# One attention block's backward pass: K read in one pass instead of two

## The chip, the cores and the metric

The kernel runs on one core of a Trainium2 chip. The core has a matrix engine (PE, with its weight loads shown apart as PEld), a vector engine (DVE), a scalar engine (ACT), a general engine (POOL) and a sync engine (SP) that issues most transfers; 16 DMA engines move data between the memory of the chip and the two on-core memories, SBUF (128 partitions) and PSUM (8 banks, the only place to which PE writes). The metric is the device time of one execution in microseconds, lower is better.

## The reference

One decode block, forward and gradient: layer norm, attention of one query per head against a cache, output projection, residual; then layer norm, a relu MLP, residual. There are B = 2 batches, H = 32 heads, Sk = 4096 cached positions, Dh = 128, D = 640, Dff = 1728, all bf16.

```python
q = (layernorm(x) @ wq).reshape(B, 1, H, Dh).transpose(0, 2, 1, 3)
scores = einsum("bhqd,bhkd->bhqk", q, k_cache) * Dh ** -0.5
o = einsum("bhqk,bhkd->bhqd", softmax(scores), v_cache)
h = x + o.transpose(0, 2, 1, 3).reshape(B, 1, H * Dh) @ wo
out = h + relu(layernorm(h) @ w1) @ w2
# returned: out, and the gradients of <out, grad_out> for x, k_cache, v_cache, wq, wo, w1, w2
```

For one batch and head write e for the unnormalised softmax weights, P = e / sum(e), go for the gradient that reaches o. The gradients of the attention are

- gV = P go' (4096 x 128),
- gs = P * (V go - dot) * scale, where dot = sum(P * (V go)), and gK = gs q' (4096 x 128),
- gq = K' gs, from which the gradients of wq and of x follow.

go depends on the whole forward pass of its batch and on the MLP's backward pass, so gV and gK can't be begun while the batch's heads are still in their forward pass. K and V of one head are 1 MiB each, gK and gV as well; there are 64 (batch, head) pairs.

## The kernel before, in words

All of K, V, gK and gV are handled pair by pair as tiles of 128 partitions x 32 columns of 128 numbers ("natural" layout, one 1 MiB transfer each). Products that sum over Dh need the transposed tile: 32 PE transposes in four groups of 8 into a PSUM bank (tag tps, two banks), each group copied to SBUF by DVE (L302) or ACT (L304). Products that sum over positions use the natural tile as the weights.

- First pass, all 64 pairs (lines 326 to 418): load K, transpose it, 32 one-column score products (L350), a softmax for four heads at a time, load V of the four heads, 32 one-column products with V (L414) that give o. Loads are issued on SP's queue.
- Change-over of a batch (`middle_gen`, lines 420 to 555): output projection, layer norm, MLP, its backward pass, and go for all heads. It is a generator, of which a few steps are run after each pair. Its long DVE work is rows of product-and-sum over wo (L549), w2 (L501) and w1 (L531).
- Second pass, all 64 pairs (lines 561 to 667): load V, transpose it, 32 one-column products with go (L593); load K again, form gs, 32 one-column products that give gq (L645); gV and gK by one DVE multiplication each (L661, L665) and a store each from POOL's queue. gV and gK have two buffers each.
- Weight gradients and the gradient of x: partly beside the second batch's second pass (`fin_wgrads_gen`), partly after the last pair (lines 817 to 847; the products of L679 are copied by L683 and L685 and stored from POOL).

```python
414    nc.tensor.matmul(ocol_ps[:, h:h + 1], lhsT=Vt[:, sc, :], rhs=P_bf[:, bh, sc:sc + 1],
                        start=(sc == 0), stop=(sc == NSC - 1))
602    nc.sync.dma_start(out=Kt[:], in_=A_k_cache[b, h].rearrange("(p sc) d -> p sc d", sc=NSC))
645    nc.tensor.matmul(gq_ps[:, h:h + 1], lhsT=Kt[:, sc, :], rhs=gs_bf[:, sc:sc + 1],
                        start=(sc == 0), stop=(sc == NSC - 1))
767    for i in range(NPAIR + LD + 1):     # first pass: pair i loads, i-1 transposes, i-2 scores, ...
792    for i in range(NPAIR + 5):          # second pass, after the whole first pass
```

The order of the work on each engine's queue is fixed when the program is built: a planner takes the instructions by their place in the program and by when it expects their inputs and buffers to be ready, so that neighbouring stages mix. A tile with n buffers can be written again when all readers of an earlier one are done; the queue that issues the transfer waits for that.

Of the kernel before, what the change touches and what calls it, by code (L numbers as in the profile page):

```python
# [12 lines left out]

EPS = 1e-5
DBG = None

MID_STEPS_PER_HEAD = 2
FIN_STEPS_PER_HEAD = 3
NDVE_FRAC = 0.72
P1_EVAC_DVE = 0.5  # L20
P2_EVAC_DVE = 0.5


def _dbg(nc, name, src_ap):
    if DBG is not None and name in DBG:
        nc.sync.dma_start(out=DBG[name], in_=src_ap)


def _chunks(total, size):
    out = []  # L30
    s = 0
    while s < total:
        n = min(size, total - s)
        out.append((s, n))
        s += n
    return out
# [3 lines left out]
def kernel(  # L40
# [26 lines left out]
    assert Sq == 1  # L67
    assert Dh == 128
    assert H * Dh == HD, "only Hq == Hkv (rep 1) supported"
    assert D % 128 == 0 and Sk % 128 == 0 and HD % 128 == 0  # L70
    assert 1 <= B <= 4
    ND = D // 128
    NSC = Sk // 128
    NF_full = Dff // 128
    F_rem = Dff - NF_full * 128
    NF = NF_full + (1 if F_rem else 0)
    PB = [32 * b for b in range(B)]
    NP = PB[-1] + 1
    SCALE = float(Dh) ** -0.5
    SCALE_BF = 0.08837890625  # L80
    eps_bf = 1.0013580322265625e-05
    NDVE = max(1, min(NSC, int(round(NSC * 0.6875))))
    GT = 8

    D_ch = _chunks(D, 512)
    F_ch = _chunks(Dff, 512)
    HD_ch = _chunks(HD, 512)

    def f_kc(c):
        return 128 if c < NF_full else F_rem  # L90

    const = ctx.enter_context(tc.tile_pool(name="const", bufs=1))
    rows = ctx.enter_context(tc.tile_pool(name="rows", bufs=1))
    cols = ctx.enter_context(tc.tile_pool(name="cols", bufs=1))
    small = ctx.enter_context(tc.tile_pool(name="small", bufs=4))
    rtmp = ctx.enter_context(tc.tile_pool(name="rtmp", bufs=1))
    ps = ctx.enter_context(tc.tile_pool(name="ps", bufs=1, space=bass.MemoryType.PSUM))
    PSB = {"tps": 2, "sps": 2, "tiny": 2, "rowps": 1, "bigps": 1, "acc": 1}
# [4 lines left out]
                            fill=1.0, base=0, pattern=[[-1, 128]], channel_multiplier=1)  # L103
    ident_f32 = const.tile([128, 128], FP32)
    nc.gpsimd.memset(ident_f32[:], 0.0)
    nc.gpsimd.affine_select(out=ident_f32[:], in_=ident_f32[:], compare_op=ALU.not_equal,
# [6 lines left out]
    x_bf = rows.tile([NP, D], BF16)  # L113
# [30 lines left out]
    for b in range(B):  # L144
        nc.sync.dma_start(out=x_bf[PB[b]:PB[b] + 1, :], in_=A_x[b, 0:1, :])
        nc.sync.dma_start(out=g_bf[PB[b]:PB[b] + 1, :], in_=grad_out[b, 0:1, :])

# [730 lines left out]
```

## Time and profile before

| | |
|---|---|
| median of 3 runs | 1195.17 us (1194.96 to 1195.88) |
| the profiled execution | 1193.57 us, span 1191.8 us |
| mean granted PE clock | 0.609 |
| packets moved | 439.78 MB, mean 369 GB/s |

Columns of a group's row: line, engine, operation, output <- inputs, shapes, count, then busy us and mean ns of one, then the engine's idle time before them and what ended it. In a row of a stretch: its bounds and length, busy time of each engine (number of instructions), the granted PE clock, the share of time in which the DMA engines were busy, GB/s. A row of a transfer gives its size and the median time from issue to landing. A row of waits gives who waited for whom, the total, how often, and the longest.

### The profile page before, as it was taken

To read this page: it belongs to the slowest core of one execution; us is meant where nothing else is said; L and a number is where in the kernel's file an instruction comes from. 1 tells how busy PE (TensorE), PEld (TensorE's weight loads), DVE (VectorE), ACT (ScalarE), POOL (GpSimd) and SP (SyncE) were. 2 spreads that over 40 slices of the span, in tenths; PEclk is the share of its full clock that TensorE was granted. 3 is DMA by queue.
4 is the path that set the end of the run, shared out by engine and by line. 5 is a ranking of instruction groups with operands and counts; after the bars stand their busy time and mean duration, and the time that the engine had idled before them with its cause. 6 is when DMAs were issued, how large, how long until landed. Compare 5 with 4: busy or idle time off the path is not lost.

```text
span 1191.8 us, 31531 instructions
## 1 busy us (share of the span) xinstructions
PE 783.3 (66%) x14044; PEld 705.3 (59%) x14044; DVE 772.4 (65%) x1622; ACT 372.3 (31%) x533; POOL 109.3 (9%) x206
## 2 busy tenths in 40 slices
PE   3966787788876667868666667545675555665245
PEld 3856677787865657767555566445664455655221
DVE  5322233235367957586987999565677788966694
ACT  1322343244333213333232223423543421322023
POOL 0100000000000000001110011010121222111111
PEclk9767778687767767555555555555755555555565
DMA  8899989988867779999999999999999999999714
GB/s 342 315 401 379 372 356 386 380 346 344 351 255 288 313 271 408 424 425 423 426 423 406 385 417 425 382 407 391 423 401 424 413 421 410 412 425 414 324 74 178
DMA packets 62097, 439.78 MB, mean 369 GB/s; under 512 B 7332, under 2 KB 7336, under 8 KB 10888
## 3 DMA queue, kind: packets, MB, share of 16 engines
q1 hardware_dynamic: 38248, 278.94, 58.1%
q0 software_dynamic: 23712, 158.81, 32.2%
q8 instruction: 110, 1.80, 0.6%
q14 instruction: 27, 0.22, 0.0%
HBM read 288.59 MB, written 149.13 MB: 367 GB/s over the span
## 4 chain that ended last, share of the span: by engine, by line
issue 22%; DMA 15%; PE 12%; DVE 12%; POOL 4%; ACT 3%; POOLq 0%; SPq 0%; ACTq 0%; DVEq 0%
DMA Vt<-in_A_v_cache_dram 7%; PE t_ps L299 6%; DMA stage<-in_A_wq_dram 5%; DVE junk L549 3%; DMA Kt<-in_A_k_cache_dram 2%; POOL out_dram L746 2%; DVE gK L665 2%; ACT VTsb L304 2%; DVE gV L661 1%; POOL out_dram L663 1%; POOL out_dram L667 1%; PE t_ps L718 1%; DVE VTsb L302 1%; PE gq_ps L645 1%; PE o_ps L679 1%
## 5 line engine op out<-in xcount | busy, mean ns | idle before, releaser
L299 PE MATMUL t_ps<-ident_bf,Vt 128*128 128x128 bf16 x2048 | 249.8, 302 | 146.9 <-ACT VTsb L304 92.8
L299 PEld LDWEIGHTS <-Vt 128*128 128x128 bf16 x2048 | 205.2, 139 | 174.6 <-issue 127.1
L299 PE MATMUL t_ps<-ident_bf,Kt 128*128 128x128 bf16 x2048 | 194.7, 255 | 63.5 <-DMA Kt<-in_A_k_cache_dram 33.4
L304 ACT COPY KTsb<-t_ps 128x1024 bf16<-128x1024 bf16 x128 | 126.2, 1013 | 241.9 <-PE t_ps L299 203.1
L299 PEld LDWEIGHTS <-Kt 128*128 128x128 bf16 x2048 | 157.3, 116 | 74.5 <-issue 35.7
L302 DVE COPY KTsb<-t_ps 128x1024 bf16<-128x1024 bf16 x128 | 88.3, 690 | 165.1 <-PE t_ps L299 163.4
L304 ACT COPY VTsb<-t_ps 128x1024 bf16<-128x1024 bf16 x128 | 129.1, 1012 | 179.6 <-PE t_ps L299 160.2
L665 DVE TENSOR_TENSOR gK<-qb,gsp 128x4096 bf16<-128x4096 bf16 x64 | 146.6, 2290 | 19.5 <-DMA out_dram<-gK 19.4
L661 DVE TENSOR_TENSOR gV<-gob,Pp 128x4096 bf16<-128x4096 bf16 x64 | 146.4, 2287 | 3.0 <-ACT gob L584 1.6
L302 DVE COPY VTsb<-t_ps 128x1024 bf16<-128x1024 bf16 x128 | 87.4, 691 | 88.8 <-PE t_ps L299 74.1
L350 PE MATMUL s_ps_g<-qcol,KTsb 128*128 128x1 bf16 x2048 | 87.8, 166 | 3.6 <-ACT KTsb L304 1.5
L645 PE MATMUL gq_ps<-gs_bf,Kt 128*128 128x1 bf16 x2048 | 69.5, 166 | 28.9 <-DVE gs_bf L628 25.3
L593 PEld LDWEIGHTS <-VTsb 128*128 128x128 bf16 x2048 | 73.2, 106 | 24.9 <-issue 22.7
L645 PEld LDWEIGHTS <-Kt 128*128 128x128 bf16 x2048 | 68.7, 105 | 32.3 <-issue 26.1
L593 PE MATMUL gp_ps<-gocol_bf,VTsb 128*128 128x1 bf16 x2048 | 73.3, 167 | 20.9 <-DVE gs L623 20.3
L414 PE MATMUL ocol_ps<-P_bf,Vt 128*128 128x1 bf16 x2048 | 62.5, 165 | 37.1 <-DMA Vt<-in_A_v_cache_dram 25.5
L414 PEld LDWEIGHTS <-Vt 128*128 128x128 bf16 x2048 | 58.5, 101 | 42.4 <-DMA Vt<-in_A_v_cache_dram 26.9
L350 PEld LDWEIGHTS <-KTsb 128*128 128x128 bf16 x2048 | 77.9, 100 | 7.5 <-ACT KTsb L304 3.5
L579 ACT CAST qb<-qb_ps 128x128 bf16<-128x128 f32 x64 | 17.1, 266 | 166.6 <-PE qb_ps L576 159.7
L663 POOL DMA_DIRECT2D out_dram<-gV x64 | 34.3, 536 | 369.8 <-DVE gV L661 258.1
L549 DVE CUSTOM_DVE_ANT_0 junk<-wo_t,gh_bcast 128x640 bf16<-128x640 bf16 x64 | 53.2, 831 | 0.5
L667 POOL DMA_DIRECT2D out_dram<-gK x64 | 34.4, 537 | 202.9 <-DVE gK L665 63.6
(180 smaller groups left out, 806.0 us busy)
## 6 DMA issues: line engine op xcount, KB each, us to landing
Kt<-in_A_k_cache_dram SPq DMA_DIRECT2D x128, 1024.0 KB, 13.9
Vt<-in_A_v_cache_dram SPq DMA_DIRECT2D x128, 1024.0 KB, 12.4
out_dram<-gV POOLq DMA_DIRECT2D x64, 1024.0 KB, 11.1
out_dram<-gK POOLq DMA_DIRECT2D x64, 1024.0 KB, 12.7
out_dram<-otile POOLq DMA_DIRECT2D x45, 160.0 KB, 10.0
wq_t<-in_A_wq_dram SPq DMA_DIRECT2D x1, 5120.0 KB, 15.3
wo_t<-in_A_wo_dram POOLq DMA_DIRECT2D x1, 5120.0 KB, 31.9
stage<-in_A_wq_dram SPq DMA_DIRECT2D x5, 1024.0 KB, 13.0
```

What stands on the lines that cost most here:

```text
L299: nc.tensor.transpose(t_ps[:, j, :], nat_tile[:, sc, :], ident_bf[:])
L302: nc.vector.tensor_copy(out=dst_sb[:, g0:g0 + gn, :], in_=t_ps[:, 0:gn, :])
L304: nc.scalar.copy(out=dst_sb[:, g0:g0 + gn, :], in_=t_ps[:, 0:gn, :])
L350: nc.tensor.matmul(s_ps[:, j, sc:sc + 1], lhsT=KTsb[:, sc, :], rhs=qcol[:, b, h:h + 1], start=True, stop=True)
L414: nc.tensor.matmul(ocol_ps[:, h:h + 1], lhsT=Vt[:, sc, :], rhs=P_bf[:, bh, sc:sc + 1], start=(sc == 0), stop=(sc == NSC - 1))
L549: nc.vector.tensor_tensor_reduce(out=junk[:], in0=wo_t[:, h, :], in1=gh1_bcast[:], scale=1.0, scalar=0.0, op0=ALU.mult, op1=ALU.add, accum ...
L593: nc.tensor.matmul(gp_ps[:, sc:sc + 1], lhsT=VTsb[:, sc, :], rhs=gocol_bf[:, b, h:h + 1], start=True, stop=True)
L645: nc.tensor.matmul(gq_ps[:, h:h + 1], lhsT=Kt[:, sc, :], rhs=gs_bf[:, sc:sc + 1], start=(sc == 0), stop=(sc == NSC - 1))
L661: nc.vector.tensor_tensor(out=gV[:].rearrange("p s (a two) -> p s a two", two=2), in0=gob3, in1=P32[:, :, None, :].to_broadcast([128, NSC, ...
L663: nc.gpsimd.dma_start(out=gV_dram, in_=gV[:])
L665: nc.vector.tensor_tensor(out=gK[:].rearrange("p s (a two) -> p s a two", two=2), in0=qb3, in1=gss[:, :, None, :].to_broadcast([128, NSC, ...
L667: nc.gpsimd.dma_start(out=gK_dram, in_=gK[:])
```

## The change

- **K is read once.** With M = V'diag(e)K (128 x 128) and u = K'e, the query gradient is gq = scale * (M' go - dot * K'e) / sum(e). Both are formed in the first pass, when K and V of the pair are in SBUF together. DVE multiplies K by e in two halves into rows of 130 numbers, the 129th being e itself; 32 products of 129 columns give M and o at once, 32 one-column products give u. M / sum(e) is kept in SBUF (tag MT, 46 buffers). The second pass no longer loads K, and gq is 32 one-column products per batch in `middle_gen`. The softmax is done for each head by itself.
- **Batches are interleaved.** Batch 0's change-over runs beside the first heads of batch 1's first pass, and as soon as its go is known, batch 0's second pass runs round by round with batch 1's first pass. What is left of batch 0's second pass runs beside batch 1's change-over, and the weight gradients run beside batch 1's second pass.
- **Buffers and queues.** V has four buffers that both passes share. gK and gV share three. wq comes in four pieces; wo, w1 and w2 are loaded by SP in six pieces between the heads. Weight gradients are outer products on PE through one PSUM bank (tag mid) and are stored from SP.
- **Layer norms and the vectors of the block** lie in columns over 128 partitions instead of in one row.

The core of the new code ("..." where lines are left out; `transpose_group` is 8 transposes and one copy, by DVE if its last argument is true and else by ACT; `matvec_group` is 8 one-column products):

```python
def load_k(i):
    Kt = work.tile([128, NSC, 128], BF16, tag="K", bufs=3, name="Kt")
    nc.sync.dma_start(out=Kt[:], in_=natural(A_k_cache, *pairs[i]))
def load_v(i):                                   # load_v2(j), of the second pass, has the same tag
    Vt = vx.tile([128, NSC, 128], BF16, tag="V", bufs=4, name="Vt")
    nc.sync.dma_start(out=Vt[:], in_=natural(A_v_cache, *pairs[i]))

def p1_iter(i):                                  # c: pair i, p: pair i-1
    c["KT0"] = transpose_group(c["K"], 0, False)
    nc.tensor.matmul(mx_ps[:], lhsT=p["rmax"][:], rhs=ident_bf[:], start=True, stop=True)
    nc.vector.reduce_max(out=gmax[:], in_=mx_ps[:], axis=AX.X)
    yield
    c["KT1"] = transpose_group(c["K"], 1, False)
    ...
    nc.scalar.activation(out=ep[:], in_=p["s"][:, :, None].to_broadcast([128, NSC, 2]),
                         func=ACT.Exp, bias=nb[:], scale=SCALE)
    yield
    matvec_group(c["s"], c.pop("KT0"), 0, q)
    c["KT2"] = transpose_group(c["K"], 2, False)
    def pk_half(k):
        pk = work.tile([128, HALF, 130], BF16, tag="pK", bufs=3, name="pk")
        sl = slice(k * HALF, (k + 1) * HALF)
        nc.vector.tensor_tensor(out=pk[:, :, 0:128]..., in0=p["K"][:, sl, :]...,
                                in1=ep[:, sl, None, :].to_broadcast([128, HALF, 64, 2]), op=ALU.mult)
        nc.vector.tensor_copy(out=pk[:, :, 128:129], in_=ep[:, sl, 0:1])
        return pk
    ...
    pk0 = pk_half(0)
    ...
    yield
    matvec_group(c["s"], c.pop("KT1"), 1, q)
    def u_half(k):
        for sc in range(k * HALF, (k + 1) * HALF):
            nc.tensor.matmul(m_ps[:, 129:130], lhsT=p["K"][:, sc, :], rhs=ep[:, sc, 0:1],
                             start=(sc == 0), stop=(sc == NSC - 1))
    u_half(0)
    yield
    pk1 = pk_half(1)
    ...
    c["KT3"] = transpose_group(c["K"], 3, True)
    yield
    ...                                          # matvec KT2, u_half(1)
    for g in range(2):
        for j in range(GT):
            sc = g * GT + j
            nc.tensor.matmul(m_ps[:, 0:129], lhsT=p["V"][:, sc, :], rhs=pk0[:, sc, 0:129],
                             start=(sc == 0), stop=False)
        yield
    ...                                          # matvec KT3, rmax, the other 16 with pk1
    nc.scalar.activation(out=MT[:], in_=m_ps[:, 0:128], func=ACT.Copy, scale=rtot[:, 0:1])
    nc.scalar.activation(out=OU[:, bp, hp, :], in_=m_ps[:, 128:130], func=ACT.Copy, scale=rtot[:, 0:1])

def p2_iter(j):                                  # c: pair j, p: pair j-1
    ...
    c["T0"] = transpose_group(c["V"], 0, False)
    nc.vector.scalar_tensor_tensor(out=gsp[:], in0=p["dp"]..., scalar=negdot[:, hp, bp:bp + 1],
                                   in1=P_bf..., op0=ALU.add, op1=ALU.mult)
    gK = work2.tile([128, NSC, 128], BF16, tag="g", bufs=3, name="gK")
    outer_half(gK, p["rb"][:, 0:128], gsp, 0)
    yield
    ...                                          # T1, T2, T3 and their products, second half of gK
    nc.gpsimd.dma_start(out=natural(out_2, bp, hp), in_=gK[:])
    ...                                          # gV, tag "g" too, in two halves, and its store

def outer_rows(pool, L, nrow, R, N, out_ap, cc): # weight gradients
    ...
    o_ps = pst([128, 512], FP32, "mid", "o_ps")
    nc.tensor.matmul(o_ps[0:P, 0:nn], lhsT=L[:, bass.ds(c0 + k, P, step=cc)], rhs=R[:, n0:n0 + nn], ...)
    ...                                          # copied by ACT and DVE in turn
    nc.sync.dma_start(out=out_v[:, c0:c0 + gn, :], in_=ot[0:P, 0:gn, :])

def interleave(gens, steps):                     # one step of each in turn, background steps behind each
    ...
                next(g)
    ...
            bg_step(steps)

for i in range(NP1 + 1):
    ...                                          # pieces of wq, wo, w1, w2
    if i + 2 < NP1: load_k(i + 2)
    if i + 1 < NP1: load_v(i + 1)
    ...
    if i == H + 1: bg.append(("m0", middle_gen(0)))
    g2 = None
    if "m0" in done and j < H:                   # go of batch 0 is known
        ...                                      # load_v2(j + 1), the first time j as well
        g2 = p2_iter(j)
        j += 1
    interleave([p1_iter(i), g2], 1)
bg.append(("m1", middle_gen(1)))
while j <= NP1:
    ...                                          # load_v2(j + 1); after m1 the weight gradients are added to bg
    interleave([p2_iter(j)], 3)
    j += 1
while bg:
    bg_step(1)
```

More of the change, by code (lines that the diff above doesn't have):

```diff
@@ L12 @@
 AX = mybir.AxisListType
[L14 to L36, printed above, removed]
 @with_exitstack
@@ L841 @@
[L841 to L847 removed]
+            bg.append(("fin", fin_gen(fin)))
+        interleave([p2_iter(j)], 3)
+        j += 1
+    while bg:
+        bg_step(1)
+    fin.release()
+    work2.release()
+    vx.release()
 _INS = ['A_x', 'A_k_cache', 'A_v_cache', 'A_wq', 'A_wo', 'B_x', 'B_w1', 'B_w2', 'grad_out']
```

1230 lines of the change are left out of this document (528 added, 702 removed).

## The prediction

> **What bounds the kernel now.** I read the page's top first: span, engines, slices, traffic.
>
> ```profile
> span 1191.8 us, 31531 instructions
> PE 783.3 (66%) x14044; PEld 705.3 (59%) x14044; DVE 772.4 (65%) x1622; ACT 372.3 (31%) x533; POOL 109.3 (9%) x206
> PEclk9767778687767767555555555555755555555565
> DMA  8899989988867779999999999999999999999714
> GB/s 342 315 401 379 372 356 386 380 346 344 351 255 288 313 271 408 424 425 423 426 423 406 385 417 425 382 407 391 423 401 424 413 421 410 412 425 414 324 74 178
> HBM read 288.59 MB, written 149.13 MB: 367 GB/s over the span
> ```
>
> No compute engine is busy more than 66%; the DMA row stands at 9 from slice 16 to 37 and the rate tops out at 423 to 426 GB/s. I use 424 GB/s as the full rate. Next the stretches: first pass, the change-over, second pass, tail (columns: PE, weight loads, DVE, ACT, POOL busy, clock, DMA share, GB/s).
>
> ```profile
> 20.00:415.00 395.00, 303.09 (x6458) 281.52 (x6456) 182.18 (x463) 136.37 (x168) 6.14 (x9) 0.74 0.86 343
> 415.00:460.00 45.00, 29.89 (x654) 26.95 (x650) 25.72 (x59) 10.38 (x20) 1.66 (x3) 0.68 0.81 318
> 460.00:1105.00 645.00, 412.49 (x6595) 378.26 (x6595) 499.85 (x999) 207.81 (x317) 89.98 (x168) 0.52 1.01 413
> 1105.00:1192.00 87.00, 36.44 (x338) 17.19 (x334) 55.89 (x78) 16.29 (x28) 10.35 (x18) 0.54 0.45 185
> ```
>
> The second pass is bound by transfers (share 1.01). The first reaches 343 GB/s, near its bound: 64 pairs in 395 us are 6.2 us each, against 2.10 MB / 424 = 4.95. The tail moves little. So a byte removed is worth time in the second pass, and only there for certain.
>
> **The change, part by part.** Per (batch, head) pair the first pass keeps K's 32 transposes, their copies and 32 score products. The 32 one-column products with V become 32 of 129 columns (V'diag(e)K and the output), and 32 one-column products of K with e are added. The second pass keeps V's 32 transposes and 32 products and loses K's load and 32 products. So K is loaded 64 times fewer: 67.1 MB less of 437.7, leaving 370.6, 874 us at 424. That is the floor; the other engines decide what of it is reached. I price PE from one stretch where the clock changes.
>
> ```profile
> 254.00:257.00 3.00, 1.11 (x23) 0.73 (x21) 0.16 (x1) 0.00 (x0) 0.00 (x0) 0.50 1.01 412
> 257.00:260.00 3.00, 3.00 (x90) 3.00 (x90) 0.00 (x0) 0.00 (x0) 0.00 (x0) 0.50 1.01 421
> 264.00:268.00 4.00, 3.44 (x80) 3.19 (x79) 1.49 (x3) 1.97 (x2) 0.00 (x0) 1.00 0.96 340
> 259.11 2.81 PE L299 MATMUL t_ps<-ident_bf,Kt 128*128 128x128 bf16 x24
> 261.72 0.40 PE L350 MATMUL s_ps_g<-qcol,KTsb 128*128 128x1 bf16 x8
> 262.94 0.61 PE L350 MATMUL s_ps_g<-qcol,KTsb 128*128 128x1 bf16 x16
> 263.41 0.67 PE L299 MATMUL t_ps<-ident_bf,Kt 128*128 128x128 bf16 x6
> 266.01 0.61 PE L299 MATMUL t_ps<-ident_bf,Kt 128*128 128x128 bf16 x8
> 266.45 0.34 PE L350 MATMUL s_ps_g<-qcol,KTsb 128*128 128x1 bf16 x8
> 275.57 0.34 PE L350 MATMUL s_ps_g<-qcol,KTsb 128*128 128x1 bf16 x8
> 275.77 0.39 PE L414 MATMUL ocol_ps<-P_bf,Vt 128*128 128x1 bf16 x10
> ```
>
> Start to start, a transpose costs (261.72-259.11)/24 = 109 ns at clock 0.5 and (266.45-266.01)/8 = 55 ns at 1.0; a one-column product (263.41-262.94)/16 = 29 and (275.77-275.57)/8 = 25 ns. The 129-column product has no row. Nearest is the transpose: 128 moving columns and a 128x128 weight load; lower end 25 ns (as if columns were free), upper end transpose plus a separate weight load, 109+29 = 138 ns. I take the transpose's. The other engines:
>
> ```profile
> L665 DVE TENSOR_TENSOR gK<-qb,gsp 128x4096 bf16<-128x4096 bf16 x64 | 146.6, 2290 | 19.5 <-DMA out_dram<-gK 19.4
> L304 ACT COPY VTsb<-t_ps 128x1024 bf16<-128x1024 bf16 x128 | 129.1, 1012 | 179.6 <-PE t_ps L299 160.2 <-DVE gss L626 9.6 <-issue 4.8
> L302 DVE COPY KTsb<-t_ps 128x1024 bf16<-128x1024 bf16 x128 | 88.3, 690 | 165.1 <-PE t_ps L299 163.4 <-PE s_ps_g L350 1.1
> L605 DVE CAST P<-P_bf 128x32 f32<-128x32 bf16 x64 | 11.1, 178 | 0.0
> L579 ACT CAST qb<-qb_ps 128x128 bf16<-128x128 f32 x64 | 17.1, 266 | 166.6 <-PE qb_ps L576 159.7 <-PE ocol_ps L414 5.4 <-DVE gs_bf L628 0.8
> L549 DVE CUSTOM_DVE_ANT_0 junk<-wo_t,gh_bcast 128x640 bf16<-128x640 bf16 x64 | 53.2, 831 | 0.5
> L501 DVE CUSTOM_DVE_ANT_0 junk<-w_t,gb_bf 128x640 bf16<-128x640 bf16 (+1 forms) x28 | 23.0, 821 | 1.9 <-DMA Kt<-in_A_k_cache_dram 1.5
> L531 DVE CUSTOM_DVE_ANT_0 junkf<-w_t,ghfbc 128x1728 bf16<-128x1728 bf16 x10 | 19.5, 1954 | 1.4 <-ACT ghfbc L523 1.2
> ```
>
> A first-pass pair then costs: PE 64x55+64x25 = 5.1 us at full clock, 64x109+64x29 = 8.8 at half; DVE 2.29 (diag(e)K in two halves, priced as gK; if rows of 130 elements halve its speed, 4.6) + 0.69 + some 8 small ones at 0.18 = 4.4; ACT 3x1.01 + 4x0.27 = 4.1; DMA 4.95. A second-pass pair: PE 32x109+32x29 = 4.4 at half clock; DVE 2x2.29 + 2 small = 4.9; ACT 4x1.01 + 2x0.27 = 4.6; DMA 3 MiB = 3.15 MB, 7.4 us.
>
> *Start:* loads and layer norm before the first head, 20 us as before (the wq load is in four pieces, hidden by the first heads).
>
> *Batch 0's first pass alone, 33 rounds.* PE is now the bound. At the 0.74 clock of the first pass half the time is at each rate: 2/(1/5.1+1/8.8) = 6.5 us; plus a tenth for waits (copies and the softmax chain have 4 us of work each beside it), 7.2 us. 33x7.2 = 238. The loads of wo, w1 and w2 (about 10 MB, 23 us) move from POOL to SP, among K and V; at 4.95 us of DMA in a 7.2 us round they are covered by 33x2.2 = 74 us of spare.
>
> *Change-over of batch 0, inside first-pass rounds.* The three product-and-sum groups are 53.2/2 + 23.0/2 + 19.5/2 = 48 us of DVE per batch, with some 70 small instructions at 0.18 61 us. It has 65 steps until its gradient is known, 11 steps a round, so 6 rounds: DVE 61+6x4.4 = 87 us.
>
> *Both passes interleaved, 26 rounds.* DMA 5 MiB, 12.4 us; PE 7.7 full, 13.3 half, 9.8 mixed; DVE 9.3; ACT 8.7. DMA bounds, if loads are issued in time. They may not be: the four V buffers now serve both passes. First-pass V is loaded a round ahead and held until its round's end, so the next second-pass V starts only when the current one has been transposed, near the middle of the round, and is wanted at the start of the next.
>
> ```profile
> Vt<-in_A_v_cache_dram SPq DMA_DIRECT2D x128, 1024.0 KB, 12.4
> out_dram<-gV POOLq DMA_DIRECT2D x64, 1024.0 KB, 11.1
> out_dram<-otile POOLq DMA_DIRECT2D x5, 432.0 KB, 2.8
> SPq L564 <- PE t_ps L299: 280.1, 45, 15.7
> PE t_ps L299 <- DMA Vt<-in_A_v_cache_dram: 42.4, 22, 4.5
> ```
>
> Today SP waits for that release (280 us in 45 times) and PE for the data 42.4 us in 22 times, 1.9 each. I add 1.6 a round: 14 us. Lower end 0; the upper is a rival, and I stay nearer to the lower because the waits in the trace are of that size. 26x14 = 364. On SP, K and first-pass V queue behind such a wait; they are wanted a round later, which covers a few us. POOL's two stores a round are no later than now; gK and gV share three buffers where they had four, and DVE waited 19.4 us in all for them, under 1 us a round.
>
> *Rest of batch 0's second pass and batch 1's change-over, 15 steps a round:* 4.3 rounds, DVE 61+4.3x4.9 = 82 us; DMA needs 32 and hides.
>
> *Batch 1's second pass with the weight gradients, 34.7 rounds.* DMA 34.7x7.4 = 257, plus 14.9 MB of weight gradients and 5.2 MB of wq, 47: 304. The gradients left the tail but their copies pass through one PSUM bank.
>
> ```profile
> 1141.53 0.60 PE L679 MATMUL o_ps<-gqf,xhat_bf 33*128 33x512 bf16 x1
> 1142.78 0.61 PE L679 MATMUL o_ps<-gqf,xhat_bf 33*128 33x512 bf16 x1
> L685 DVE CAST otile<-o_ps 128x512 bf16<-128x512 f32 x20 | 13.8, 692 | 11.3 <-PE o_ps L679 11.2
> ```
>
> One product and its copy took 1.25 us; 160 of them and some 40 row pieces, at 1.45 with engines shared, are 290; 20 wq groups at two copies' time 40. Their stores move from POOL to SP, where each waits for its copies and holds the V loads behind it; with one pass left the four buffers put those loads some three rounds (22 us) ahead, so I cost that at nothing, and a whole round of 7.4 if a store came last. 330 us, a little over the 304, so I take 330 and the tail of 87 is inside it.
>
> Sum: 20+238+87+364+82+330 = 1121, and 1.8 around the span (the profiled run took 1193.57): 1123 us, against 1193.57 of that run; the median of the runs, 1195.17, is 1.6 higher.
>
> **The rivals.**
>
> *PE stays at clock 0.5.* The second pass ran at 0.52, with PE idle a third of the time. The change moves one-column work into wide work, and gaps for copies could hold the clock down. Then 33 rounds cost 8.8x1.1 = 9.7, 2.5 more, 82 us; 26 rounds 15 instead of 14, 26 us: 1231. Against it: 257:260 is wholly busy at 0.5 and by 264 the clock is 1.0, though 24 transposes filled most of it. [...]
>
> *The second-pass V comes late (the slower side).* Place: the 26 interleaved rounds. A megabyte sharing the rate with one store needs 2.1/424 = 4.9 us, plus 1.8 for issue and completion (the 432 KB stores landed in 2.8 us, of which 0.44/0.424 = 1.0 is data), and if nothing is left of the round when it starts PE stands 7 us, 5.4 more than I counted: 26x5.4 = 140, 1263. It turns to slower from 2.8 us more a round (72/26). For: SP's waits above. Against: second-pass transposes come in the first half of the round.
>
> *PE warm, no V wait.* Denser PE keeps the clock at 1.0: 33 rounds at 5.7, 50 us less; 26 rounds at 12.4, 42 less; gradients hidden, 18 less: 1013.
>
> *The removed load was hidden anyway.* The second pass at share 1.01 speaks against it; it would leave the time near 1195 only if the added PE work exactly repaid it.
>
> **How the numbers follow.** Forecast, 1060 to 1185: 0.50. Warm PE: 0.17. Late V: 0.16. Slow clock: 0.12. Near 1195 from a mixture: 0.05, within which 0.03 lies inside 0.2% (2.4 us; the three runs span 0.9). Faster: 0.50+0.17+0.01 = 0.68; slower: 0.16+0.12+0.01 = 0.29. Range 1013 to 1263, the ends of the warm and late cases; beyond lie little more than tails.
>
> **What would show it.** K read once: HBM read near 221 MB. PE bound: first rounds near 7.2 us, DMA share about 0.7. Interleaved rounds: 14 us, share about 0.9, PE waiting for V 1 to 2 us each. Change-overs: DVE full for some 60 us each. After batch 1's change-over: share near 1, no tail of 80 us. Wrong would be: rounds of 9 us or more in the first pass at clock 0.5, PE waits of 4 us or more for V, or weight gradients running on alone after the last gK.

## The result and the profile after

The changed kernel takes 1161.03 us (median of 4 runs, 1155.89 to 1165.52), before 1195.07 beside it; the ratio is 0.9717, interval 0.9673 to 0.976. Faster, as forecast, but by 34 us where 72 were forecast. The profiled execution took 1162.05 us.

The top of its page (the same rows as shown of before):

```profile
span 1160.3 us, 31933 instructions
PE 867.1 (75%) x14099; PEld 734.9 (63%) x14099; DVE 718.3 (62%) x1492; ACT 602.3 (52%) x914; POOL 69.9 (6%) x137
PEclk9799888995855877888788877665755555555555
DMA  9699997884741999999999998960499997999972
GB/s 353 268 394 357 355 363 283 324 332 156 273 155 56 384 393 376 384 382 393 387 373 385 393 363 343 364 259 0 187 389 422 398 372 303 399 373 382 376 289 109
HBM read 221.48 MB, written 149.13 MB: 319 GB/s over the span
```

67 MB less are read (221.48 against 288.59). But the mean rate fell from 367 to 319 GB/s, and the rate row shows where: 156, 273, 155 and 56 GB/s in slices 10 to 13 and 259, 0, 187 in 27 to 29. Cut into its stages (columns: PE, weight loads, DVE, ACT, POOL busy with counts, clock, DMA share, GB/s), the span reads: start and batch 0's first pass; batch 0's change-over, from its first row to go known; both passes interleaved; batch 1's change-over; its second pass; what follows the last gV.

```profile
20.00:257.00 237.00, 211.65 (x4272) 194.88 (x4271) 129.36 (x327) 125.60 (x224) 0.00 (x0) 0.91 0.89 337
257.00:368.00 111.00, 70.98 (x1241) 65.32 (x1241) 79.28 (x228) 34.25 (x62) 0.11 (x1) 0.65 0.45 166
384.00:702.00 318.00, 248.59 (x4537) 232.62 (x4536) 199.18 (x369) 187.50 (x277) 24.52 (x46) 0.81 0.98 380
712.00:824.00 112.00, 40.91 (x723) 36.02 (x721) 83.48 (x198) 30.50 (x41) 6.93 (x13) 0.58 0.52 208
824.00:1117.00 293.00, 245.20 (x2651) 172.31 (x2649) 184.13 (x274) 190.87 (x263) 33.05 (x62) 0.55 0.94 371
1117.00:1160.00 43.00, 16.95 (x32) 3.57 (x30) 15.29 (x28) 8.20 (x14) 1.07 (x2) 0.50 0.42 171
```

| stage | predicted | measured |
|---|---|---|
| start, batch 0's first pass | 20 + 238 | 257 |
| change-over of batch 0 | 87 | 111 |
| interleaved | 364 (26 rounds) | 344 (25 rounds, 368 to 712) |
| change-over of batch 1 | 82 | 112 |
| batch 1's second pass, gradients, tail | 330 | 336 |
| sum | 1121 | 1160 |

The two change-overs are 54 us over, the rest 15 under. In both, the transfers stand half idle (shares 0.45 and 0.52). What PE does there (a row of the waits: who for whom, total, times, longest):

```profile
PE rb_ps L528 <- DVE goc L480: 56.6, 2, 28.3
```

And the timeline of after around the first of the two (start, duration, engine, line, and in brackets the idle time before):

```profile
339.10 0.82 DVE L397 CUSTOM_DVE_ANT_0 junk<-wo_t,hbc 128x640 bf16<-128x640 bf16 x1 [2.58 <-ACT hbc L384]
...
366.84 0.19 DVE L480 CAST goc<-go 128x32 bf16<-128x32 f32 x1
367.08 0.29 PE L528 MATMUL rb_ps<-ident_bf,goc 128*128 128x128 bf16 x1 [28.32 <-DVE goc L480]
```

From 339.1 to 366.8 DVE works through the 32 sums over wo (0.82 us each, back to back), and PE stands 28.3 us at the product that spreads go of the first pair of the second pass: it stands in PE's fixed order ahead of first-pass work that could run. With what must be refilled afterwards, no first-pass round ends between 339 and 383. In batch 1's change-over the same row costs another 28.3, and there nothing is left to run: the last gV of batch 0 starts at 763.9, the next at 824.3.

Batch 0's change-over has three parts:

```profile
257.00:290.00 33.00, 30.89 (x629) 29.12 (x628) 12.15 (x47) 14.46 (x24) 0.00 (x0) 0.64 0.50 181
290.00:339.00 49.00, 39.21 (x603) 35.46 (x603) 40.12 (x116) 19.34 (x38) 0.11 (x1) 0.72 0.62 233
339.00:368.00 29.00, 0.89 (x9) 0.73 (x10) 27.01 (x66) 0.45 (x2) 0.00 (x0) 0.53 0.10 36
```

In the first, PE is the engine that is nearly full, at clock 0.64 where it had 1.00 just before (199 to 256); 300 one-column products of the change-over itself (projection and MLP) stand among those of the rounds. In the last, DVE works and PE has nothing. In batch 1's change-over DVE stands 12.3 us for stores, because gV and gK share three buffers:

```profile
DVE gV L513 <- DMA out_dram<-gK: 9.1, 4, 4.0
DVE gK L513 <- DMA out_dram<-gV: 3.2, 2, 1.8
```

### The profile page after: what moved, and what is told of

Its sections match the earlier page's. It is cut to its first block, busy times and chain, and to the rows that moved or that the text cites. A ratio compares the mean times of both kernels' runs of the same rounds, so it can differ in the third digit from the quotient of the medians.

```text
span 1160.3 us, 31933 instructions
## 1 busy us (share of the span) xinstructions
PE 867.1 (75%) x14099; PEld 734.9 (63%) x14099; DVE 718.3 (62%) x1492; ACT 602.3 (52%) x914; POOL 69.9 (6%) x137
## 3 DMA queue, kind: packets, MB, share of 16 engines
HBM read 221.48 MB, written 149.13 MB: 319 GB/s over the span
## 4 chain that ended last, share of the span: by engine, by line
issue 40%; PE 26%; DVE 13%; DMA 9%; ACT 8%; POOL 4%; POOLq 0%; SPq 0%; DVEq 0%; ACTq 0%
PE t_ps L243 8%; DMA out_dram<-gK 7%; DVE junk L397 7%; ACT t_sb L248 6%; PE m_ps L362 4%; PE m_ps L349 4%; PE s_ps L254 3%; PE o_ps L599 3%; POOL out_dram L563 2%; DVE gV L513 2%; POOL out_dram L549 2%; DVE ot L605 1%; DMA Vt<-in_A_v_cache_dram 1%; DVE pk L305 1%; PE m_ps L326 1%
## 5 line engine op out<-in xcount | busy, mean ns | idle before, releaser
L248 ACT COPY t_sb<-t_ps 128x1024 bf16<-128x1024 bf16 x458 | 454.1, 1013 | 212.0 <-PE t_ps L243 205.8
L243 PE MATMUL t_ps<-ident_bf,Vt 128*128 128x128 bf16 x2048 | 243.0, 279 | 25.6 <-DMA Vt<-in_A_v_cache_dram 20.4
L243 PEld LDWEIGHTS <-Vt 128*128 128x128 bf16 x2048 | 173.3, 125 | 55.6 <-issue 27.2
L254 PEld LDWEIGHTS <-t_sb 128*128 128x128 bf16 x4096 | 162.7, 103 | 63.9 <-ACT t_sb L248 35.4
L513 DVE TENSOR_TENSOR gV<-rb,pp 128x2048 bf16<-128x2048 bf16 x128 | 153.3, 1213 | 46.5 <-DMA out_dram<-gK 43.7
L513 DVE TENSOR_TENSOR gK<-rb,gsp 128x2048 bf16<-128x2048 bf16 x128 | 154.2, 1217 | 30.0 <-DMA out_dram<-gV 29.1
L305 DVE TENSOR_TENSOR pk<-Kt,ep 128x2048 bf16<-128x2048 bf16 x128 | 155.1, 1212 | 25.8 <-ACT ep L294 25.6
L349 PE MATMUL m_ps<-pk,Vt 128*128 128x129 bf16 x1024 | 105.3, 254 | 12.4 <-DVE pk L309 12.4
L254 PE MATMUL dp_ps<-goc,t_sb 128*128 128x1 bf16 x2048 | 95.5, 167 | 7.6 <-ACT t_sb L248 5.6
L254 PE MATMUL s_ps<-qc,t_sb 128*128 128x1 bf16 x2048 | 90.3, 165 | 10.4 <-ACT t_sb L248 6.9
L362 PE MATMUL m_ps<-pk,Vt 128*128 128x129 bf16 x1024 | 90.2, 232 | 1.9 <-DVE pk L309 1.9
L349 PEld LDWEIGHTS <-Vt 128*128 128x128 bf16 x1024 | 80.2, 114 | 13.6 <-issue 13.6
L362 PEld LDWEIGHTS <-Vt 128*128 128x128 bf16 x1024 | 68.5, 104 | 2.4 <-issue 2.4
L326 PE MATMUL m_ps<-ep,Kt 128*128 128x1 bf16 x2048 | 61.6, 164 | 0.0
L528 PE MATMUL rb_ps<-ident_bf,goc 128*128 128x128 bf16 x64 | 16.8, 267 | 56.6 <-DVE goc L480 56.6
## 6 DMA issues: line engine op xcount, KB each, us to landing
wo_t<-in_A_wo_dram SPq DMA_DIRECT2D x4, 1280.0 KB, 11.3
```

The source lines that it names most:

```text
L243: nc.tensor.transpose(t_ps[:, j, :], nat[:, g * GT + j, :], ident_bf[:])
L248: nc.scalar.copy(out=t_sb[:], in_=t_ps[:])
L254: nc.tensor.matmul(dst[:, sc:sc + 1], lhsT=t_sb[:, j, :], rhs=vec, start=True, stop=True)
L305: nc.vector.tensor_tensor(out=pk[:, :, 0:128].rearrange("p s (a two) -> p s a two", two=2), in0=p["K"][:, sl, :].rearrange("p s (a two) -> ...
L326: nc.tensor.matmul(m_ps[:, 129:130], lhsT=p["K"][:, sc, :], rhs=ep[:, sc, 0:1], start=(sc == 0), stop=(sc == NSC - 1))
L349: nc.tensor.matmul(m_ps[:, 0:129], lhsT=p["V"][:, sc, :], rhs=pk0[:, sc, 0:129], start=(sc == 0), stop=False)
```

## The experiments

Each time is a median of 4 to 10 executions; the ratio is to the kernel before, run beside it. e4_narrow and e7_m1 leave out part of the result, the others compute all of it. "Hole" is a stretch in which no gV starts, read from the timeline.

| run | us (range) | ratio to before (interval) |
|---|---|---|
| after | 1161.03 (1155.89–1165.52) | 0.9717 (0.9673–0.976) |
| e1_late | 1130.47 (1119.81–1134.29) | 0.9453 (0.9405–0.9502) |
| e2_passes | 1133.39 (1128.81–1139.1) | 0.9486 (0.9444–0.9529) |
| e3_banks | 1174.73 (1168.27–1177.88) | 0.9832 (0.9798–0.9865) |
| e4_narrow | 1080.51 (1076.55–1085.47) | 0.9051 (0.9021–0.9082) |
| e5_banks2 | 1146.17 (1142.46–1149.83) | 0.9597 (0.9571–0.9622) |
| e6_room | 1122.03 (1116.79–1126.09) | 0.9393 (0.9357–0.943) |
| e7_m1 | 1183.26 (1180.13–1185.83) | 0.9906 (0.9886–0.9926) |
| e8_both | 1134.92 (1133.97–1142.23) | 0.9516 (0.9485–0.9547) |
| e9_q | 1205.46 (1204.14–1206.66) | 1.0093 (1.0077–1.0109) |
| e10_q8 | 1155.43 (1148.71–1157.01) | 0.9663 (0.9632–0.9694) |
| e11_q | 1252.74 (1244.53–1256.81) | 1.0466 (1.0427–1.0505) |
| e12_lead | 1201.24 (1198.01–1202.55) | 1.0056 (1.0037–1.0075) |
| e13_splead | 1119.36 (1116.41–1125.44) | 0.9389 (0.9353–0.9426) |
| e14_rb | 1195.29 (1189.63–1198.94) | 0.9995 (0.9976–1.0014) |
| e15_rbsp | 1114.66 (1112.26–1117.6) | 0.9325 (0.9302–0.9348) |
| e16_fin24 | 1079.95 (1078.19–1088.96) | 0.9066 (0.9038–0.9095) |

### Are the change-overs the loss? e4_narrow, e1_late, e2_passes

**e4_narrow**: the change-overs' sums run over 64 columns only, so the gradients stay incomplete.

```diff
- nc.vector.tensor_tensor_reduce(out=junk[0:kc, 0:width], in0=in0, in1=in1, ...
+ nc.vector.tensor_tensor_reduce(out=junk[0:kc, 0:64], in0=in0[:, 0:64], in1=in1[:, 0:64], ...
```

> The product-and-sum instructions of the change-overs run over 64 columns only instead of 640 and 576, so gradients are left incomplete; DVE's time in them falls from about 49 us to about 10 in each batch. If the change-overs stand on the path with nothing beside them (theory W), the whole of the last part (28 us each) and part of the earlier ones comes off: 60 to 80 us less, about 1090. If they are covered by the rounds beside them, at most 20 us less, 1140 or more.

The change-overs of its trace:

```profile
257.00:330.00 73.00, 65.75 (x1180) 61.20 (x1180) 43.06 (x227) 30.40 (x56) 0.11 (x1) 0.68 0.61 223
673.00:744.00 71.00, 38.05 (x723) 33.17 (x719) 47.96 (x198) 30.72 (x42) 6.41 (x12) 0.68 0.80 315
```

They are 38 and 41 us shorter than the 111 and 112 of after, 79 together, and the time fell by 80.5. DVE is busy 36 us less in each. So DVE's sums are on the path for their full length; nothing beside them takes the time up. The prediction had them on the path too, so this run alone doesn't show what it had wrong.

**e1_late**: batch 0's second pass begins with round 45 only.

```diff
- if "m0" in done and j < H:
+ if "m0" in done and i >= 45 and j < H:
```

> The second pass of batch 0 begins at round 45 of the first pass instead of round 39, six rounds after its gradient is known in program order. Theory W (the change-overs are bare waits: PE's queue stands at the product that broadcasts go, 28.3 us once and a gap of 60.4 us between two gV later): the first wait is filled by first-pass rounds and twelve pairs instead of six are left to cover batch 1's change-over, so some 28 + 40 us go, about 1095 us. Rival O (the change-overs cost what DVE works in them, whatever lies beside): the order changes nothing, 1155 to 1165 us. Rival R (the interleaved rounds are what is too slow): six rounds fewer are interleaved and their work is done apart at the same sum, 1150 to 1170.

```profile
257.00:386.00 129.00, 109.64 (x1944) 101.22 (x1942) 96.08 (x279) 54.02 (x98) 0.11 (x1) 0.73 0.60 220
386.00:657.00 271.00, 221.24 (x3963) 206.01 (x3963) 172.29 (x325) 161.90 (x241) 20.87 (x39) 0.77 0.95 369
657.00:796.00 139.00, 66.50 (x1135) 59.01 (x1133) 111.66 (x237) 55.68 (x73) 13.32 (x25) 0.62 0.78 305
```

The first hole is gone: PE is busy 110 us of 129 in batch 0's change-over, and the two stages up to batch 1's change-over take 400 us where they took 455. That isn't all gain: 20 pairs of the second pass are begun by then, where after had begun 26. Batch 1's change-over grew from 112 to 139, since 12 of batch 0's pairs share DVE with it instead of 6, and a hole of 36 us is left at its end (760 to 796), with PE's wait of 28.3 us for goc as before. The whole gained 31 us. The result lies between the two theories: the first wait is filled, as theory W had it, the second is not.

**e2_passes**: no interleaving; the second pass follows the first.

```diff
- if "m0" in done and j < H:
+ if False:
```

> K is read once, but the second pass of batch 0 begins only when the first pass of both batches is done. Theory W: nothing on PE's queue waits for go of batch 0, and batch 1's change-over lies beside 32 pairs of batch 0. First pass 64 rounds at 7.1 us plus some 30 us for batch 0's change-over in it, second pass 32 pairs at 8 and 32 at 9, little tail: 257+258+256+290+10 = about 1070 us. Rival I (interleaving is what brings the gain, because PE's work lies beside transfers): 25 rounds lose an overlap of several us each, 1200 us or more. Rival O: the DVE work of the change-overs is paid as before, 1150 or more.

28 us faster than with interleaving: neither theory's number. The first pass alone ends at 529. The following 19 pairs, which run beside batch 1's change-over, cost 8.9 us each where the bytes alone would need 7.4 at 424 GB/s:

```profile
540.00:690.00 150.00, 84.89 (x1271) 73.67 (x1270) 127.49 (x247) 75.05 (x94) 18.06 (x34) 0.63 0.94 361
```

An interleaved round of 13.8 us saves 2.4 us against one of each pass apart (7.3 and 8.9, the latter beside the change-over's sums), 60 us in 25 rounds. Against it stand the holes that come with the interleaving, 45 and 60 us: batch 0's change-over waits for its first pair, and batch 1's finds batch 0's pairs used up. e2_passes has one hole, of 33 us (697 to 730). That reckoning, 105 less 33 less 60, gives 12 of the 28 us; where the others come from isn't shown.

### Clock and width: e7_m1

The 32 products of 129 columns have one column only, in both halves, so M is left out; the copy that fills MT stays, but reads pk.

```diff
- nc.tensor.matmul(m_ps[:, 0:129], lhsT=p["V"][:, sc, :], rhs=pk0[:, sc, 0:129],
+ nc.tensor.matmul(m_ps[:, 128:129], lhsT=p["V"][:, sc, :], rhs=pk0[:, sc, 128:129],
```

> The changed kernel with the 32 products of V'diag(e)K cut to their last column, so that only the output is formed and the query gradient is left wrong; weight loads, DVE's multiplication of K and the number of instructions stay. A first-pass round at clock 1.0 took 6.41 us. If the columns cost what a transpose's do (55 ns against 25), 32 x 30 ns = 1 us goes, rounds of 5.4 us; 33 rounds 30 us less; the interleaved rounds, at a DMA share of 0.99, stay at 13.8. About 1130 us. If the softmax chain sets the rounds, nothing goes: 1155 or more. If PE also sets the interleaved rounds: another 30 us or more less, below 1105.

A miss: 22 us slower with less to do. The same stretch of the first pass, of after:

```profile
199.00:256.00 57.00, 52.97 (x1174) 48.74 (x1174) 35.97 (x90) 35.25 (x63) 0.00 (x0) 1.00 0.89 329
```

and of e7_m1:

```profile
199.00:256.00 57.00, 45.66 (x909) 42.50 (x907) 27.41 (x68) 27.87 (x49) 0.00 (x0) 0.53 0.68 257
```

PE gets through 1174 products at clock 1.0, and through 909 lighter ones at 0.53. Start to start (medians of that stretch) a 129-column product is 59 ns, a transpose 56 and a one-column product 25 in after; in e7_m1 the transpose is 106 and a one-column product 27. The round is 8.4 us instead of 7.1. The run changes the width of these products and with it all the work that PE has; it can't say which of the two the clock follows.

### Where the weight gradients stand: e3_banks, e5_banks2, e8_both

The gradients' products (L599) go through one PSUM bank, each some 1.6 us after the last (median of after). **e3_banks** gives them a second tag.

```diff
- o_ps = pst([128, 512], FP32, "mid", "o_ps")
+ o_ps = pst([128, 512], FP32, ("mid", "m")[fw[0] % 2], "o_ps")
```

> The weight gradients' products use two PSUM banks in turn instead of one. If the tail (some 40 us after the last gV) is the chain of product and copy through one bank, the gradients end earlier and most of it goes: 1120 to 1130 us. If the pace is set by the engines that copy or by the steps given to the gradients in each round, nothing moves: 1158 to 1165.

The gradients ended at 1016 instead of 1153, and the kernel became 14 us slower: no gV starts between 949 and 1027. SP's waits in 945 to 1030:

```profile
SPq L608 <- DVE ot L605: 70.1, 10, 17.3
```

and the stretch:

```profile
945.00:1025.00 80.00, 53.66 (x266) 24.67 (x265) 28.65 (x53) 36.60 (x62) 1.06 (x2) 0.50 0.46 180
```

SP stands 70 of these 80 us at ten stores of weight gradients, each waiting for its copies, and the V load of the next pair stands behind them in the queue. **e5_banks2** also takes two background steps instead of three once the gradients run; **e8_both** is e5_banks2 with e1_late's edit.

```diff
- interleave([p2_iter(j)], 3)
+ interleave([p2_iter(j)], 3 if fin is None else 2)
```

> Two PSUM banks for the weight gradients, as in the run before, and two background steps instead of three behind each step of the second pass once they run. With three steps the gradients ended at 1016 us, but no gV was begun from 949 to 1027: with two banks always ready, they were placed ahead of the second pass on every queue and held its loads back. If that is the cause, spreading them over more rounds removes that hole and leaves no chain after the last gV: 1115 to 1130 us. If the slower time came from sharing the bank m itself, it stays at 1165 to 1180.

> The later second pass of e1_late (1130 us) with the two banks and two steps of e5_banks2. Both act on different stretches, so their gains add: 1130 less some 40 us of tail, about 1090. If the tail's work comes back as slower second-pass rounds (DVE and ACT copy the gradients there), 1120 or more.

The first came out between its two cases, the second at the worse. Each has the hole again: 1017 to 1060 in e5_banks2, 921 to 998 in e8_both. SP's timeline in e8_both:

```profile
900.71 0.33 SPq L505 DMA_DIRECT2D Vt<-in_A_v_cache_dram  x1
905.23 0.33 SPq L627 DMA_DIRECT2D wqs<-in_A_wq_dram  x1
909.11 77.33 SPq L608 DMA_DIRECT2D out_dram<-ot  x11
```

and its stretch:

```profile
921.00:998.00 77.00, 52.49 (x319) 23.72 (x318) 27.98 (x49) 37.47 (x61) 0.87 (x2) 0.54 0.41 161
```

Eleven stores in a row, then the next V load. Two gains that each were real (31 and 15 us) gave 26 together.

### Room, and a queue of V's own: e6_room, e9_q to e12_lead, e14_rb

**e6_room** is e2_passes with the first pass's room released before the second pass: six gV/gK buffers instead of three, and MT in the pool that stays.

```diff
+ work.release()
+ work2 = tc.alloc_tile_pool(name="work2", bufs=1, side="right")
  bg.append(("m1", middle_gen(1)))
...
- gK = work2.tile([128, NSC, 128], BF16, tag="g", bufs=3, name="gK")
+ gK = work2.tile([128, NSC, 128], BF16, tag="g", bufs=6, name="gK")
```

> The passes one after the other as in e2_passes (1133 us), with K's room given to gK and gV: six buffers instead of three. The second pass alone took 8.9 us a pair there, against 7.4 for its bytes at 424 GB/s, and DVE waited for stores of gK and gV to land. If three buffers hold DVE and the store queue back, pairs take about 7.8: 60 us less, 1075. If DVE's work (the change-over's sums beside the second pass) or the loads set the pace, no more than 15 us less, 1118 or more.

```profile
539.00:691.00 152.00, 94.56 (x1457) 84.41 (x1454) 137.16 (x265) 78.04 (x99) 20.33 (x38) 0.59 0.95 389
691.00:726.00 35.00, 26.25 (x332) 19.31 (x333) 13.49 (x32) 18.50 (x27) 1.06 (x2) 0.65 0.59 218
```

A pair costs 8.0 instead of 8.9, 11 us in all; the sum is that of the expectation's second case. Then comes a hole of 35 us, and a row of SP's waits that names it:

```profile
SPq L627 <- DVE go L397: 35.8, 1, 35.8
```

SP stands 35.8 us at the first slice of wq, whose room is that of wo, read by the last of the sums; V's loads stand behind. **e9_q** issues the second pass's V loads from POOL; **e10_q8** does so in e8_both; **e11_q** is e9_q with two banks.

```diff
- nc.sync.dma_start(out=Vt[:], in_=natural(A_v_cache, *pairs[j]))
+ nc.gpsimd.dma_start(out=Vt[:], in_=natural(A_v_cache, *pairs[j]))
```

> e6_room with one edit: the V loads of the second pass are issued from POOL instead of SP. In e6_room's trace SP stands 35.8 us at the load of wq's first slice (it waits for the room that wo held, until the last sum over wo), and the V loads that follow it in SP's queue stand behind it: no gV between 691 and 726, where a pair takes 8.5. Theory Q (the hole is the V loads standing in a shared queue): the hole closes, 35 less one period, about 27 us off 1122: 1090 to 1100. Rival P (the hole is DVE's or PE's own order, the sums over wo go ahead of the pairs whichever queue brings V): 1115 or more, the hole stays. A cost of its own: POOL now has three transfers to issue per pair and a V load can stand behind a store that waits for DVE; if that decides, over 1130.

> e8_both (second pass of batch 0 from round 45 on, gradients over two banks, two steps per yield) with the same edit, V loads of the second pass from POOL. In e8_both SP stands 75.2 us at stores of the weight gradients, 11 of them one after the other between 909 and 986, with the next V load behind them; no gV between 921 and 998. Theory Q: these 77 us shrink to some 10, so 1135 - 65 = about 1070 (up to 1090 if the gradients then run on at the end). Rival P (PE and DVE take the gradients' steps first in their own fixed order): no change, 1125 to 1140. The gap in front of batch 1's first pair, which waits for goc (36 us in e1_late), stays in both.

> e9_q with the outer products of the weight gradients alternating between two PSUM tags. Two banks made the time longer in e3_banks, where SP then stood 70 us at the gradients' stores with V loads behind. Theory Q: with V loads on another queue this loss is gone; the pairs beside the gradients are then set by DVE and the transfers (8 us a pair in e6_room before the gradients, 9.2 with them, some 30 pairs), so equal to e9_q or up to 25 us less. Rival: two banks cost something else (PE's order), then slower than e9_q by 20 or more.

The holes closed in e9_q and e10_q8 (no gap between two gV is above 23 us), and both became slower, by 83 and 20 us. e11_q has a hole of 119 us (730 to 849) and is 131 slower than e6_room, although V has a queue of its own there. POOL stood in it:

```profile
POOL Vt L505 <- PE t_ps L243: 109.0, 1, 109.0
```

The V load waits for PE to transpose an earlier V and free its buffer, while PE works through 116 products of the weight gradients (L599). So with two banks PE's own order can make the hole too, as the rival of e11_q's expectation had it; for e3_banks and e5_banks2 no run separates the two, and for e8_both only e10_q8 speaks for the queue. e9_q's time is in the range of the third case of its expectation, but that loads behind stores in POOL's queue set it isn't shown. In e9_q, beside the gradients and after them:

```profile
760.00:960.00 200.00, 156.35 (x1385) 99.99 (x1381) 112.38 (x166) 116.20 (x167) 28.18 (x53) 0.53 0.87 327
1000.00:1100.00 100.00, 52.51 (x690) 45.81 (x691) 55.58 (x65) 44.43 (x53) 16.48 (x31) 0.53 0.90 334
```

A pair takes 11.3 and 9.4 us (9.0 in e6_room beside the gradients), and no engine is full: PE is busy 78% at most, the transfers 0.87 and 0.90. **e12_lead** asks for each V one pair earlier, **e14_rb** gives in addition five buffers to the row copies rb.

```diff
- LEAD = 1
+ LEAD = 2
...
- rb = work2.tile([128, 256], BF16, tag="rb", bufs=3, name="rb")
+ rb = work2.tile([128, 256], BF16, tag="rb", bufs=5, name="rb")      # e14_rb, e15_rbsp
```

> e9_q (V loads of the second pass on POOL) with each V load asked for one pair earlier (two ahead instead of one, the same four V buffers). In e9_q's trace a V load is issued right behind the gV store, 0.53 us after it, and its own pair's gV store comes two periods of 12.1 us later: load 8.6, transposes and products until 9 later, sums of gK and gV 5: a loop with two loads in it. Theory F (too few loads in flight): three loads in the loop make 24.2/3 = 8.1 us a pair, up to the 9.2 that e6_room has beside the gradients: 64 pairs from 534 on at 8.1 to 9.2, tail 20: 1075 to 1145, and the hole stays closed. Rival (the pairs are limited by PE or POOL themselves and the loads wait for it): no change, 1190 to 1210.

> e12_lead with five buffers of the row copies rb instead of three. In e12_lead's steady state (1050 to 1070) nothing is full: gK's sums end at 1060.7, then rb's copy 1060.81 on ACT, then PE's rb_ps 1061.23, 16 transposes from 1061.40, products until 1067.5, gsp, gK's sums from 1067.8: one closed chain of 9.4 us a pair. Theory R (the ring of three rb buffers closes the chain): 93 us of PE's waits go, a pair falls to what the transfers allow (8.0 in e6_room), 64 pairs from 537 on at 8 to 9: 1070 to 1130. Rival (the order on the queues closes it, or the transfers of one queue do): no change, 1185 to 1205.

Neither depth nor the ring is it: 4 and 6 us. One period of e12_lead's timeline shows what a pair consists of:

```profile
1058.10 0.28 DVE L538 SCALAR_TENSOR_TENSOR gsp<-dp_ps,negdot,P_bf 128x64 bf16<-128x64 f32 x1 [4.22 <-PE dp_ps L254]
1058.41 2.36 DVE L513 TENSOR_TENSOR gK<-rb,gsp 128x2048 bf16<-128x2048 bf16 x2
1060.81 0.37 ACT L531 CAST rb<-rb_ps 128x256 bf16<-128x256 f32 x1 [3.18 <-DVE gK L513]
1061.23 0.26 PE L526 MATMUL rb_ps<-ident_bf,qsc 128*128 128x128 bf16 x1 [3.17 <-ACT rb L531]
1061.40 1.91 PE L243 MATMUL t_ps<-ident_bf,Vt 128*128 128x128 bf16 x16
...
1067.09 0.37 PE L254 MATMUL dp_ps<-goc,t_sb 128*128 128x1 bf16 x8 [0.69 <-ACT t_sb L248]
1067.49 0.28 DVE L538 SCALAR_TENSOR_TENSOR gsp<-dp_ps,negdot,P_bf 128x64 bf16<-128x64 f32 x1 [4.22 <-PE dp_ps L254]
```

gK's product, rb's copy, rb_ps, the transposes, the products, gsp, gK's product: a closed chain of 9.4 us, in which a pair's transposes begin only when the pair before has its gK. From 760 to 1100 this wait of rb's copy for gK adds up to 23.0 us in e6_room and to 49.8 in e9_q. That the planner placed the work otherwise once the load had moved is an inference; no run tests it. Why rb's copy waits for that gK with five buffers as with three stays open, and so does the cause of the 83 and 20 us.

### The hole by position: e13_splead, e15_rbsp, e16_fin24

V on SP again. **e13_splead** is e6_room with LEAD = 2, **e15_rbsp** adds the five rb buffers, **e16_fin24** lets the weight gradients, and so wq's slices, begin at pair 24.

```diff
- if "m1_end" in done and fin is None:
+ if "m1_end" in done and fin is None and j >= 24:
```

> e6_room with each V load asked for one pair earlier, on SP as before. Theory F and theory Q together: one more V tile is there when SP stops at wq's slice, so the hole of 35 us loses one period of 8.5, and the rest stays: about 1113. Rival 1 (depth helps every pair): pairs below 8 us, under 1100. Rival 2 (the fourth buffer isn't free so early, SP waits for it): 1120 to 1125.

> e13_splead (V loads on SP, two pairs ahead) with five rb buffers. There PE waits 46.6 us for rb's copy in 16 times. Theory R: some of these lie in the stretch with DVE full (19 pairs at 8 us, transfers at 418 GB/s), where nothing is to be had, the rest beside the gradients: 10 to 25 us less than 1119. Rival: no change within 6 us, as the transfers (0.97 to 1.0 busy at 390 to 424 GB/s from 750 to 1100) take up the slack.

> e15_rbsp, with the weight gradients allowed from pair 24 of the second pass on, so that the loads of wq's slices stand behind more V loads in SP's queue and the room of wo is free when SP comes to them. Theory Q: SP doesn't stand 35.8 us, gV runs through the end of the change-over at 8 to 9 us a pair, and 36 - 8 = some 27 us go: 1115 - 27 = 1088 (1080 to 1098), if the gradients, which ended 46 us ahead of the last gV, keep within it. Rival S (DVE's sums over wo hold the pairs, the queue only looks guilty): the hole stays, 1108 to 1120. Rival T (the later gradients outlast the pairs): hole gone, last gV earlier, but a tail behind it and 1100 or more.

The first two gain 3 and 5 us, near what a run varies by, and keep the hole (684 to 720, 686 to 722). The third gains 35, and its hole is gone (gV at 686, 693, 698, 703). SP's timeline there:

```profile
680.20 8.89 SPq L505 DMA_DIRECT2D Vt<-in_A_v_cache_dram  x2
691.71 1.01 SPq L627 DMA_DIRECT2D wqs<-in_A_wq_dram  x2
697.52 20.08 SPq L505 DMA_DIRECT2D Vt<-in_A_v_cache_dram  x4
```

and its second pass in two stretches:

```profile
533.00:693.00 160.00, 111.43 (x1713) 98.77 (x1711) 144.59 (x278) 94.42 (x120) 20.86 (x39) 0.65 0.98 398
693.00:1064.00 371.00, 306.49 (x3346) 216.14 (x3345) 253.72 (x373) 239.18 (x326) 45.83 (x87) 0.56 1.00 407
```

SP's waits in 640 to 760 have 2.6 us for wo's last sum instead of 35.8. The gradients' products themselves hardly moved (714 to 1048, in e15_rbsp 708 to 1046), so what changed, as far as the trace shows, is the place of wq's loads among V's. From 693 to the last gV the transfers are busy throughout, at 407 GB/s. This is the fastest version that computes everything: 1079.95 us, 81 less than the change as made and 114 less than before.

## Why the prediction was right or wrong

- **Direction and bytes: right.** HBM read is 221.48 MB against "near 221 MB", and the time fell.
- **Start and batch 0's first pass: right, with compensating parts.** 257 us against 258. The wide product, which had no row, is 59 ns against the transpose's 55 that was taken. The clock was 0.91 against an assumed 0.74, and the rounds 7.1 against 7.2: at clock 1.0 a round came to 6.4 us, not 5.7. The rows of 130 numbers did not slow DVE: half a tile took 1212 ns (L305), half of gK 1217 (L513). That the sum met was luck in part. The DMA share was 0.89, not the 0.7 that the prediction named as a sign.
- **The two change-overs: the step that failed.** The prediction put "DVE 61+6x4.4 = 87 us" and 82: DVE's work of the change-over and of the rounds beside it, as if DVE were always fed. Its work was near that, 79 and 83 us busy, but the change-overs took 111 and 112: DVE stood 32 and 29 us, which less the 7 by which its work fell short is the 54 us they are over. In batch 0's, PE's and DVE's work came one after the other: PE was busy 94% from 257 to 290 at clock 0.64, with the change-over's own 300 products, which the prediction left at nothing, and empty from 339, since the product at L528 waits for go ahead of the first-pass work in PE's order. In batch 1's, DVE stood 12.3 us for stores of gK and gV, which the prediction put at under 1 us a round, and some 13 for the chain's own small products and broadcasts; the pairs ran out before the chain did. e4_narrow shows that nothing beside the chain takes up DVE's sums (80.5 us off for 79 us shorter change-overs), e1_late that the first hole comes from where the second pass begins, e6_room that buffers for gK and gV are worth some 11 us when the passes follow each other. What the 300 products and the lower clock cost, no run isolates.
- **Interleaved rounds: right in the sum, wrong in the cause.** 13.8 us against 14.0, but these were to be 12.4 us of transfers at 424 GB/s and 1.6 of waits for V. The transfers were busy 0.98 at 380 GB/s, which for 5 MiB is the 13.8 itself. This row, over the whole kernel, leaves half of the forecast waits for V, 20.4 us (all of them in this stage) against 26x1.6 = 42. That the two errors met at 13.8 is luck; why the rate stays at 380 there, no run shows. The row:

```profile
L243 PE MATMUL t_ps<-ident_bf,Vt 128*128 128x128 bf16 x2048 | 243.0, 279 | 25.6 <-DMA Vt<-in_A_v_cache_dram 20.4
```

- **Last second pass and tail: right in size.** 336 against 330. The chain through one PSUM bank sets the end, as priced: with two banks (e3_banks) the gradients ended 137 us earlier. But one of the prediction's own signs of being wrong came: the gradients ran on for 32 us after the last gK (1120 to 1153), in a tail of 43. The stores ahead of V's loads, "I cost that at nothing", cost little here: SP stood at them 74.6 us in all from 824 to 1117, in 12 waits of at most 23.4, and no two gV lie more than 15 us apart. With the chain shortened, 38 to 75 us of such waits lay in one stretch, and gV stopped (e3_banks, e5_banks2, e8_both).
- **Rivals.** V late: 20.4 us in all against 140 more. The slow clock didn't come: 0.91 and 0.81 in the PE-heavy stages. Without the width of the products that this change adds it came (e7_m1: 0.53 from 199 to 256, where after has 1.00); transposes are over half of PE's work there (32 x 106 ns against 96 x 27 a round). Before's first pass, which has as many transposes and no wide product, ran at 0.78 (150 to 200). The stretch that the prediction holds against this rival doesn't decide it, and is not mostly transposes: 81 one-column products (256.95 to 259.25) stand ahead of the 24, which have 0.9 of the 3 us from 257 to 260. So no run here settles what the clock follows. Warm PE came for some rounds only (1.0 from 199 to 256), and denser PE did not always have it: busy without a break from 264 to 272, PE ran at 0.50.

## What to carry to other kernels

A stage with a serial chain on one engine is cut into stretches by which engine is full in each, and priced by its chain, plus whatever is first in each queue and waits for the chain's end: PE stood 28.3 us at L528 in each change-over of after, and in batch 0's the first-pass work behind it in the fixed order covered nothing of that. A load behind another transfer that waited in the same queue was late by that wait (35.8 us in e6_room), and asking for it a pair earlier left the hole (36 us in e13_splead): look at which transfer the issuing queue stands at, and move that one later in the program (35 us less in e16_fin24) before giving the load a queue of its own (83 us more in e9_q, for a reason that stayed open). Speeding up a stage that paces stores on a shared queue cost more than it gained in e3_banks (14 us).

## What the runs showed of the hardware

- Less work on PE was slower (e7_m1, 199 to 256): with one column instead of 129 in a quarter of the first pass's products the clock was 0.53 where after had 1.0, and transposes took 106 ns start to start instead of 56, while PE was busy 80% instead of 93%. Before ran at 0.78 with PE busy 81% (150 to 200), and in after PE was busy without a break from 264 to 272 at clock 0.50, some 7 us after the change-over's one-column products had begun among the round's. So the busy share alone doesn't give the clock of these stretches.
- A DMA share near 1.0 was not one rate: 380 GB/s in the interleaved stage of after (share 0.98), 407 in e16_fin24's second pass (1.00), 413 over the second pass of before (1.01) and up to 426 in single slices of it. At 424 GB/s an interleaved round's bytes come to 12.4 us, and it took 13.8: a floor from bytes depends on the stage whose rate it takes. Whether the mix of loads and stores sets the rate, no run shows.
